# Attention and SwiGLU block: the low part of the first chunk's row maxima is made by an accumulated TensorE product, and the later units' subtract stands farther from its neighbours

## The chip, the cores and the metric

The kernel runs on one core of one Trainium2 chip. Its engines work side by side, each in the order of its own instructions: TensorE (PE, with its weight loads as PEld), VectorE (DVE), ScalarE (ACT), GpSimd (POOL) and SyncE (SP, which here only starts DMAs). The metric is the device time of one execution in microseconds (us), as the median of several runs.

## What is computed

A transformer block over 2048 tokens of width 512: adaptive layer norm, attention with 32 heads of 16 values each and a full softmax, and a SwiGLU feed-forward of width 1792, each with a gated residual.

```python
mod = (_silu(c) @ w_mod).reshape(c.shape[0], 6, 1, -1)
sa, ca, ga, sb, cb, gb = (mod[:, 0], mod[:, 1], ..., mod[:, 5])
h = _layernorm(x) * (1 + ca) + sa
q, k, v = split_heads(h @ wqkv)              # H = 32, Dh = 16
p = _softmax(einsum("bhqd,bhkd->bhqk", q, k) * Dh ** -0.5)
x = x + ga * (merge_heads(p @ v) @ wo)
h = _layernorm(x) * (1 + cb) + sb
x = x + gb * ((_silu(h @ w_gate) * (h @ w_up)) @ w_down)
```

The weights are scaled so that scores are large; the softmax subtracts each row's maximum, and products are made from a high and a low part of each operand (a value rounded to TensorE's fp32r format, and the rest), which keeps about full fp32 accuracy.

## The kernel before

**Units and steps.** The 2048 queries are four chunks of 512. A unit is one chunk and one group of four heads, so there are 32 units, 8 to a chunk; the first chunk's are units 0 to 7. A unit has 16 steps, one for each tile of 128 keys, and a step has four pairs. A pair (`pair_of`) is one score product of the current unit (L512, 128 keys by 512 queries, into one PSUM bank), its exponential on ScalarE (L514), and one product for a later unit's maxima (L482, 128 queries by 512 keys), of which VectorE takes the row maximum (L484). The maxima run 23 steps (`LEAD`) ahead of the scores. After a step follow the products with V (L527).

**The maxima of a unit.** When all 64 row maxima of unit u are there, `max_rows(u)` runs. A small reduce on VectorE (L489) brings the four key parts together into the tile `m`, 128 by 16. ScalarE rounds `m` into the first half of `nm` (L501), VectorE subtracts the rounded value from `m` into the second half (L502). Both inputs of this subtract lie in SBUF. TensorE turns the 32 columns into rows and negates them by a product with `minus`, a negated identity (L494); ScalarE copies the rows out (`mr`, L496), and two DMAs on SP's queue (L498) put them into rows 48 and 49 of the operand `qop` of unit u. The operand `kop` holds ones there, so the score product subtracts the maximum by itself, as a high and a low part.

**What sets the order.** There is no scheduler here: the order is written out by hand. `max_rows` appends its later pieces to the list `side`, and each pair takes one piece off it after its own products; `wait` is an empty piece. So the number of empty pieces is the distance, in pairs, between the reduce, ScalarE's rounding, the subtract and the row product. The last piece appends the row product to `tails`, which is emptied by `flush`. In the part written by `plain` that is after every three pairs (`WIN`); in the part written by `filled`, where feed-forward products (L733) are placed between the pairs, it is after a block of 10 or 5 pairs.

**The stages.** Until about 200 us the projections are made. Then come 144 plain steps (`STARTS[0]`), in which the first chunk's units are done; only units 1 to 8 are of interest there, since the maxima run ahead. In these steps GpSimd also splits the weights of the feed-forward and of `wo` into high and low parts (`split_weights`, L585 to L593 and L611, L627): it loads them, works on tiles of 128 by 512 or 1024 and stores them by DMA. After that the output projection and feed-forward of the chunks before are filled in between the pairs.

**SP's queue** takes its DMAs in order, and each waits for what it needs: the rows (L498), key operands (`kop<-kd`, L414), query operands (`qop<-qd`, L414), the softmax denominators (L538 to L548) and the feed-forward weights (`wgu<-gu_dr`, L668).

Of the kernel before, what the change touches and what calls it, by code (L numbers as in the profile page):

```python
# [9 lines left out]
F32 = mybir.dt.float32  # L10
# [4 lines left out]
ALU = mybir.AluOpType  # L15
AX = mybir.AxisListType
# [3 lines left out]
P = 128  # L20
# [7 lines left out]
NC = 4  # L28
# [9 lines left out]
LEAD = 23  # L38
# [4 lines left out]
UG = 16 * NG  # L43
# [61 lines left out]
def block_kernel(ctx, tc, x, wqkv, wo, w_gate, w_up, w_down, c, w_mod, out):  # L105
    nc = tc.nc
# [27 lines left out]
    ident = const.tile([P, P], F32, name="ident")  # L134
    eps_t = const.tile([P, 1], F32, name="eps_t")
    minus = const.tile([P, P], F32, name="minus")
# [322 lines left out]
    pb = ctx.enter_context(tc.tile_pool(name="pb", bufs=2, reuse_waits="tile"))  # L459
    kop[1] = [pb.tile([P, 2, CW], F32R, name=f"kop1{c}", bufs=1) for c in range(NC)]  # L460
    pf = None
    nms = [pb.tile([P, 2, 16], F32R, name=f"nm{e}", bufs=1) for e in range(2)]
    qop, mx, pts, pv, o_, due, res = {}, {}, {}, {}, {}, {}, {}
    posts, tails = [], []
    n = 16 * NU
# [19 lines left out]

    def max_rows(u):

        m = pb.tile([P, 16], F32, name="m", tag="m")
        nc.vector.tensor_reduce(m, mx.pop(u).rearrange("p b s t f -> p (b s t) f"), op=ALU.max, axis=AX.X)  # L489
        nm = nms[u % 2]  # L490

        def rows():
            pr = bank("pr")[0:32, 0:P]
            nc.tensor.matmul(pr, nm.rearrange("p r h -> p (r h)").bitcast(F32), minus, start=True, stop=True)  # L494
            mr = pb.tile([32, P], F32R, name="mr", tag="mr", bufs=1)
            nc.scalar.copy(mr, pr)  # L496
            for r in range(2):
                nc.sync.dma_start(qop[u][KR + r:KR + r + 65:64].bitcast(F32), mr[16 * r:16 * r + 16, :].bitcast(F32))  # L498

        wait = lambda: None  # L500
        side.extend([wait] * 3 + [lambda: nc.scalar.copy(nm[:, 0, :], m), wait,  # L501
                                  lambda: nc.vector.tensor_sub(nm[:, 1, :].bitcast(F32), m, nm[:, 0, :].bitcast(F32)),  # L502
                                  wait, lambda: tails.append(rows)])

    def score(i, h):
        u, kt = divmod(i, 16)
# [318 lines left out]
    side = []  # L825
# [61 lines left out]
    def after(i):  # L887
        nonlocal pf
        for f in due.pop(i, []):
            f()  # L890
        j = i + LEAD
        if j % 16 == 15 and j < n:
            max_rows(j // 16)
        if i == -2:
            run(late)
            sm.finish()
            es_a0.close()
            pf = ctx.enter_context(tc.tile_pool(name="pf", bufs=1, side="right", reuse_waits="tile"))
            load_q(2)
        if 0 <= i < UG and i % 16 in (3, 5, 8):  # L900
            next(weights2, None)
# [195 lines left out]
```

## Time and profile before

| what | us |
| --- | --- |
| median of 3 runs (1903.62 to 1907.65) | 1906.04 |
| the profiled execution | 1910.84 |
| its span | 1909.1 |
| L484 on DVE, 2048 row maxima, busy | 1261.8 |
| L482 on PE, their products, busy | 788.5 |
| L512 on PE, the score products, busy | 744.4 |

The span is what the profiler saw from the first to the last instruction; the profiled execution's time holds another 1.74 us around it. A group's row in the profile names the line of the code, the engine, the operation, what it writes and reads, the count, and then busy time, mean duration of one in ns, and idle time of the engine just ahead of it with what ended it. A row of the timeline is start, duration, engine, line. A row of windows is the stretch, its length, and then the busy time of an engine in it with the number of instructions, the clock granted to TensorE (1.00 is full), the share of the DMA engines and their GB/s.

### The profile page before, as it was taken

How to read it: one execution, taken by the hardware profiler on the slowest of the kernel's cores; microseconds unless marked ns; L12 is line 12 of the kernel's file. 1: busy time of each engine (PE TensorE's matmuls, PEld its weight loads, DVE VectorE, ACT ScalarE, POOL GpSimd, SP SyncE). 2: the span in 40 equal slices, each digit the busy share in tenths (PEclk: the TensorE clock that was granted, in tenths of full speed). 3: DMA queues.
4: the chain of work that ended last, by engine and by line, in shares of the span. 5: the costliest groups of instructions: out<-in, count | busy, mean ns of one | idle time of the engine just before them, and what ended most of it. 6: DMA issues, size and time to landing. Idle time of an engine off the chain costs nothing.

```text
span 1909.1 us, 42023 instructions
## 1 busy us (share of the span) xinstructions
PE 1861.7 (98%) x16872; PEld 1209.6 (63%) x16872; DVE 1492.1 (78%) x2515; ACT 1253.3 (66%) x2406; POOL 486.1 (25%) x528
## 2 busy tenths in 40 slices
PE   7999999999999999999999999999999999999999
PEld 5766444444455677777765677766664677666887
DVE  5459999999998888888888888888788888821543
ACT  4221888787786777777777777777777777784211
POOL 3000544454501222212232222222223222232200
PEclk9999999998999999999999999999999999999999
DMA  8854555554432433333244333333242433333543
GB/s 280 289 210 131 183 179 177 160 172 157 156 130 68 132 116 124 116 111 120 92 146 120 105 112 115 122 119 120 79 131 77 148 116 111 118 124 143 195 182 109
DMA packets 101787, 266.97 MB, mean 140 GB/s; under 512 B 20360, under 2 KB 25480, under 8 KB 88408
## 3 DMA queue, kind: packets, MB, share of 16 engines
q1 hardware_dynamic: 86984, 202.27, 33.4%
q0 software_dynamic: 14608, 62.01, 9.2%
q8 instruction: 133, 2.18, 0.5%
q14 instruction: 62, 0.51, 0.1%
HBM read 201.46 MB, written 61.86 MB: 138 GB/s over the span
## 4 chain that ended last, share of the span: by engine, by line
PE 78%; DVE 20%; ACT 1%; DMA 1%; issue 0%; SPq 0%; ACTq 0%; DVEq 0%
PE bank L527 19%; PE bank L733 18%; DVE mx L484 17%; PE bank L512 14%; PE bank L482 9%; PE bank L742 7%; PE bank L219 7%; DVE nm L502 1%; PE bank L775 1%; DMA kop<-kd 0%; PE bank L172 0%; DMA wm_ab<-in_w_mod 0%; PE bank L494 0%; PE bank L718 0%; DVE stt L758 0%
## 5 line engine op out<-in xcount | busy, mean ns | idle before, releaser
L484 DVE TENSOR_REDUCE mx<-bank 128x1 f32<-128x512 f32 x2048 | 1261.8, 682 | 199.6 <-PE bank L482 153.4
L482 PE MATMUL bank<-kop,qop 48*128 48x512 f32 x2048 | 788.5, 446 | 4.8 <-DMA qop<-qd 1.6
L512 PE MATMUL bank<-qop,kop 50*128 50x512 f32 x2048 | 744.4, 424 | 4.6 <-DVE mx L484 2.6
L512 PEld LDWEIGHTS bank<-qop,kop 50*128 50x128 f32 x2048 | 352.4, 187 | 245.6 <-issue 40.3
L482 PEld LDWEIGHTS bank<-kop,qop 48*128 48x128 f32 x2048 | 348.5, 186 | 70.4 <-DVE mx L484 15.4
L733 PE MATMUL bank<-act,wgu 64*128 64x512 f32 x1872 | 353.9, 398 | 0.0
L733 PEld LDWEIGHTS bank<-act,wgu 64*128 64x128 f32 x1872 | 228.2, 186 | 20.7 <-ACT part L808 4.1
L733 PE MATMUL bank<-wd,mid 64*128 64x512 f32 x912 | 151.4, 394 | 0.0
L809 POOL TENSOR_TENSOR x<-part,x 128x512 f32<-128x512 f32 x76 | 96.4, 1287 | 194.3 <-ACT part L808 194.3
L554 POOL TENSOR_TENSOR on<-o,rb 128x512 f32<-128x512 f32 x31 | 39.8, 1285 | 362.4 <-DMA rb<-d_dr 318.1
L794 POOL CAST mid<-m 128x512 fp32r<-128x512 f32 x40 | 24.4, 610 | 352.6 <-PE bank L482 198.7
L733 PEld LDWEIGHTS bank<-wd,mid 64*128 64x128 f32 x912 | 97.9, 186 | 13.5 <-DVE m L792 2.0
L219 PE MATMUL bank<-hT,wqs 128*128 128x512 f32 x384 | 96.1, 400 | 2.3 <-ACT hT L338 1.0
L790 DVE SCALAR_TENSOR_TENSOR q<-th,bank 128x512 f32<-128x512 f32 x56 | 38.1, 681 | 72.1 <-ACT th L786 72.1
L219 PEld LDWEIGHTS bank<-hT,wqs 128*128 128x128 f32 x384 | 70.3, 188 | 24.2 <-issue 6.0
L786 ACT ACTIVATE th<-bank 128x512 f32<-128x512 f32 x56 | 33.5, 598 | 77.8 <-PE bank L742 65.9
L379 DVE TENSOR_TENSOR prt<-bank,prt 128x512 fp32r<-128x512 f32 x32 | 22.0, 689 | 46.8 <-ACT prt L377 42.7
L377 ACT CAST prt<-bank 128x512 fp32r<-128x512 f32 x32 | 18.8, 587 | 59.7 <-PE bank L219 52.8
L792 DVE TENSOR_TENSOR m<-bank,q 128x512 f32<-128x512 f32 x56 | 38.7, 692 | 24.5 <-PE bank L742 21.6
L742 PE MATMUL bank<-act,kop 128*128 128x512 f32 x240 | 57.2, 396 | 0.0
L733 PE MATMUL bank<-wgu,act 64*128 64x512 f32 x288 | 55.0, 397 | 0.1
L742 PE MATMUL bank<-wd,mid 128*128 128x512 f32 x216 | 52.3, 395 | 0.3 <-DVE mid L795 0.3
(6276 smaller groups left out, 5198.7 us busy)
## 6 DMA issues: line engine op xcount, KB each, us to landing
kop<-kd SPq DMA_DIRECT2D x256, 192.0 KB
wgu<-gu_dr SPq DMA_DIRECT2D x46, 1024.0 KB
wd<-wd_dr SPq DMA_DIRECT2D x28, 1024.0 KB
gu_dr<-wgu POOLq DMA_DIRECT2D x14, 1024.0 KB, 5.4
qop<-qd SPq DMA_DIRECT2D x64, 192.0 KB
kop<-gu_dr SPq DMA_DIRECT2D x20, 512.0 KB
kd<-prt SPq DMA_DIRECT2D x16, 512.0 KB
qd<-prt SPq DMA_DIRECT2D x16, 512.0 KB
```

The costliest lines, as they stand in the source:

```text
L219: nc.tensor.matmul(pt, lhs(a, k), rhs(b, k), start=(n == 0), stop=(n == 3 * nk - 1))
L482: nc.tensor.matmul(pm, qop[u][rows, s, qt * P:(qt + 1) * P], kop[u % 2][kc][rows, s, :], start=True, stop=True)
L484: nc.vector.tensor_reduce(mx[u][:, b, s, qt, kc:kc + 1], pm, op=ALU.max, axis=AX.X)
L512: nc.tensor.matmul(sp, kop[u % 2][kt // 4][rows, h // 2, kt % 4 * P:(kt % 4 + 1) * P], qop[u][rows, h // 2, :], start=True, stop=True)
L527: nc.tensor.matmul(pv[u][32 * h:32 * h + 32, cols], v_flat[:, e0:e0 + 32], p_[h][:, cols], start=(kt == 0 and half == 0), stop=(kt == 15), ...
L554: mul.tensor_mul(on, o, rb)
L733: nc.tensor.matmul(outs[e], lhs(e, a, k)[rows], rhs(b, k)[rows], start=(ph == 0 and j == 0), stop=(ph == 1 and j == z))
L742: nc.tensor.matmul(outs[e], lhs(e, a, k), rhs(b, k), start=(j == 0), stop=(j == z))
L786: nc.scalar.activation(th, outs[0], AF.Tanh, scale=0.5)
L790: nc.vector.scalar_tensor_tensor(q, th, 1.0, outs[0], op0=ALU.add, op1=ALU.mult)
L792: nc.vector.tensor_mul(m32, outs[1], q)
L809: nc.gpsimd.tensor_add(ch.x2[:, t, :], part, ch.x2[:, t, :])
```

## The change

For units 0 to 8 (`early`), the subtract on VectorE is left out. The reduce writes `m` twice, side by side (128 by 32, its input read twice); ScalarE writes the rounded value into the second half of `nm`, whose first half is zero from two memsets ahead; and TensorE accumulates two products into the same rows, `m` by `minus` and `nm` by `ident`. So the first 16 rows are minus the maximum, the others the rounded value less the maximum. For units 9 to 31 the subtract stays; ScalarE's rounding and the subtract stand one pair earlier, and the row product one pair later.

```diff
     nms = [pb.tile([P, 2, 16], F32R, name=f"nm{e}", bufs=1) for e in range(2)]
+    for t in nms:
+        nc.vector.memset(t[:, 0, :].bitcast(F32), 0.0)
...
-        m = pb.tile([P, 16], F32, name="m", tag="m")
-        nc.vector.tensor_reduce(m, mx.pop(u).rearrange("p b s t f -> p (b s t) f"), op=ALU.max, axis=AX.X)
+        m = pb.tile([P, 2, 16], F32, name="m", tag="m")
+        by_head = mx.pop(u).rearrange("p b s t f -> p (b s t) f")[:, None]
         nm = nms[u % 2]
+        early = 16 * u + 15 - LEAD < UG
+        wait = lambda: None
...
-            nc.tensor.matmul(pr, nm.rearrange("p r h -> p (r h)").bitcast(F32), minus, start=True, stop=True)
+            parts = ((m, minus), (nm.bitcast(F32), ident)) if early else ((nm.bitcast(F32), minus),)
+            for k, (a, by) in enumerate(parts):
+                nc.tensor.matmul(pr, a.rearrange("p r h -> p (r h)"), by, start=k == 0, stop=k == len(parts) - 1)
...
-        wait = lambda: None
-        side.extend([wait] * 3 + [lambda: nc.scalar.copy(nm[:, 0, :], m), wait,
-                                  lambda: nc.vector.tensor_sub(nm[:, 1, :].bitcast(F32), m, nm[:, 0, :].bitcast(F32)),
-                                  wait, lambda: tails.append(rows)])
+        if early:
+            nc.vector.tensor_reduce(m, by_head.to_broadcast([P, 2, 16, NC]), op=ALU.max, axis=AX.X)
+            side.extend([wait] * 3 + [lambda: nc.scalar.copy(nm[:, 1, :], m[:, 0, :])] + [wait] * 3)
+        else:
+            nc.vector.tensor_reduce(m[:, 0, :], by_head[:, 0], op=ALU.max, axis=AX.X)
+            side.extend([wait] * 2 + [lambda: nc.scalar.copy(nm[:, 0, :], m[:, 0, :]), wait,
+                                      lambda: nc.vector.tensor_sub(nm[:, 1, :].bitcast(F32), m[:, 0, :],
+                                                                   nm[:, 0, :].bitcast(F32))] + [wait] * 3)
+        side.append(lambda: tails.append(rows))
```

VectorE's order at unit 4, before: `mx` is the tile of maxima, the banks are those of the L482 products, and the tile `nm_974` is `nm` of the even units.

```order
L489 TENSOR_REDUCE m<-mx 128x16
L484 TENSOR_REDUCE mx<-bank_65 128x1
L484 TENSOR_REDUCE mx<-bank_66 128x1
L484 TENSOR_REDUCE mx<-bank_63 128x1
L484 TENSOR_REDUCE mx<-bank_64 128x1
L484 TENSOR_REDUCE mx<-bank_65 128x1
L484 TENSOR_REDUCE mx<-bank_66 128x1
L502 TENSOR_TENSOR nm_974<-m,nm_974 128x16
L484 TENSOR_REDUCE mx<-bank_63 128x1
```

And the same place in the changed kernel, where the maxima's line is L486 and the small reduce's is L507:

```order
L507 TENSOR_REDUCE m<-mx 128x32
L486 TENSOR_REDUCE mx<-bank_65 128x1
L486 TENSOR_REDUCE mx<-bank_66 128x1
L486 TENSOR_REDUCE mx<-bank_63 128x1
L486 TENSOR_REDUCE mx<-bank_64 128x1
L486 TENSOR_REDUCE mx<-bank_65 128x1
L486 TENSOR_REDUCE mx<-bank_66 128x1
L486 TENSOR_REDUCE mx<-bank_63 128x1
```

The subtract is gone, and the row maxima of the next products follow each other without it; the small reduce writes 32 columns in place of 16. On TensorE, the row product of unit 4 before stands behind the last product of a window and ahead of the products with V (L527):

```order
L512 MATMUL bank_69<-qop,kop_973 128x512
L482 MATMUL bank_65<-kop_970,qop 128x512
L494 MATMUL bank_67<-minus,nm_974 32x128
L527 MATMUL bank_70<-pt__3263,v_flat 32x256
```

In the changed kernel the score product's line is L523, the row product's L500 and the products with V are L538:

```order
L523 MATMUL bank_69<-qop,kop_973 128x512
L484 MATMUL bank_65<-kop_970,qop 128x512
L500 MATMUL bank_67<-minus,m 32x128
L500 MATMUL bank_67<-ident,nm_974 32x128
L538 MATMUL bank_70<-pt__3265,v_flat 32x256
```

The place is the same; there are two row products, and neither reads anything that a subtract wrote. In the filled part the extra pair moves the row product of units 15 and 23 past the end of a block, by 10 pairs, and that of unit 30 by 5; the other units' stay where they were. On SP's queue at unit 15, before, the rows (`qop<-mr`) go ahead of a weight load and two key operands:

```order
L548 DMA rb<-d_dr 128x1x512
L498 DMA qop<-mr 2x8x128 x2
L668 DMA wgu<-gu_dr 128x2048
L414 DMA kop_89<-kd 48x2x512 x2
L414 DMA kop_90<-kd 48x2x512 x2
```

In the changed kernel (L559 is the denominators' broadcast, L679 the weight load, L504 the rows):

```order
L559 DMA rb<-d_dr 128x1x512
L679 DMA wgu<-gu_dr 128x2048
L414 DMA kop_89<-kd 48x2x512 x2
L504 DMA qop<-mr 2x8x128 x2
L414 DMA kop_90<-kd 48x2x512 x2
```

The rows go behind the weight load and the first key operand now. GpSimd's order is unchanged.

## The prediction

> **What bounds the kernel now.** I read the page first, then the stage in which the removed instruction stands, cut into units.
>
> ```profile
> span 1909.1 us, 42023 instructions
> ...
> PEclk9999999998999999999999999999999999999999
> ...
> PE 78%; DVE 20%; ACT 1%; DMA 1%; issue 0%; SPq 0%; ACTq 0%; DVEq 0%
> PE bank L527 19%; PE bank L733 18%; DVE mx L484 17%; PE bank L512 14%; PE bank L482 9%; PE bank L742 7%; PE bank L219 7%; DVE nm L502 1%; PE bank L775 1%; DMA kop<-kd 0%; PE bank L172 0%; DMA wm_ab<-in_w_mod 0%; PE bank L494 0%; PE bank L718 0%; DVE stt L758 0%
> ```
>
> On the whole TensorE sets the end (78% of the chain of waits), but a fifth of the chain is VectorE's, nearly all of it row maxima (L484). Two things stand out: the subtract L502, 32 instructions of 128 by 16, has 1% of the chain, and the granted clock, full elsewhere, has a lower tenth in the first quarter of the span. In the chain in order of time, VectorE's long pieces stand between 200 and 560 us, such as
>
> ```profile
> 306.15 27.00 DVE mx L484 x45
> ...
> 344.13 3.11 DVE nm L502
> ```
>
> So I cut that stretch at the starts of the small reduce L489, from unit 1's at 219.73 to unit 9's at 553.58: each window is one unit's worth of pairs, and holds the subtract of the unit whose reduce opens it. This is VectorE in each, with the clock behind the count:
>
> ```profile
> 219.73:257.88 38.15, 38.15 (x67) 1.00 0.42 129
> 257.88:297.94 40.06, 39.92 (x68) 1.00 0.68 209
> 297.94:340.34 42.40, 42.32 (x70) 1.00 0.58 176
> 340.34:383.86 43.52, 41.46 (x67) 0.96 0.55 171
> 383.86:423.85 39.99, 39.85 (x68) 1.00 0.57 184
> 423.85:471.80 47.95, 43.23 (x69) 0.86 0.49 156
> 471.80:514.46 42.66, 40.15 (x68) 0.92 0.50 166
> 514.46:553.58 39.12, 38.99 (x68) 1.00 0.44 146
> sum 333.85, DVE 324.07; mean DVE 40.51
> ```
>
> The reader is to see that VectorE is busy for 324 of 333.85 us, so it sets the pace here, and that the units should be alike but last from 38.2 to 48.0 us. The same windows for the subtract alone, four of them and the sum:
>
> ```profile
> 219.73:257.88 38.15, 0.33 (x1) 1.00 0.42 129
> 257.88:297.94 40.06, 1.83 (x1) 1.00 0.68 209
> ...
> 383.86:423.85 39.99, 1.76 (x1) 1.00 0.57 184
> ...
> 514.46:553.58 39.12, 0.90 (x1) 1.00 0.44 146
> sum 333.85, DVE 15.77; mean DVE 1.97
> ```
>
> One subtract takes 2 us on the mean. The timeline of unit 4 shows why:
>
> ```profile
> 344.04 0.78 POOL L585 DMA_DIRECT2D mid<-in_B_w_up  x1
> 344.05 3.18 DVE L502 TENSOR_TENSOR nm<-m,nm 128x16 f32<-128x16 f32 x1
> 344.83 2.36 POOL L627 TENSOR_TENSOR mid<-mid,gb_bc 128x1024 f32<-128x1024 f32 x1
> 347.15 1.28 DVE L484 TENSOR_REDUCE mx<-bank 128x1 f32<-128x512 f32 x2
> ...
> 347.37 0.35 PE L494 MATMUL bank<-minus,nm 128*32 128x128 f32 x1 [3.19 <-DVE nm L502]
> ```
>
> The subtract begins beside GpSimd's work and ends at 347.23, 0.04 us after GpSimd's L627 (347.19): it was held by it. VectorE's queue stands behind it, and TensorE, which has reached the row product L494, waits 3.19 us. Then the clock falls, here behind the subtracts of units 4, 6 and 7:
>
> ```profile
> 348.00:352.00 4.00, 4.00 (x34) 0.65 0.35 69
> ...
> 432.00:436.00 4.00, 4.00 (x25) 0.50 0.49 143
> ...
> 480.00:484.00 4.00, 4.00 (x26) 0.51 0.61 216
> ```
>
> At half the clock TensorE no longer feeds VectorE, which idles in turn:
>
> ```profile
> L484 DVE TENSOR_REDUCE mx<-bank 128x1 f32<-128x512 f32 x511 | 309.0, 680 | 9.7 <-PE bank L482 7.8 <-PE bank L512 1.4
> ```
>
> **The change, part by part.** *The subtract of units 1 to 8 goes.* I take its worth from whole units, since it also brings the idle time after it. The four units at full clock throughout, less their subtract, last 38.15 - 0.33 = 37.82, 40.06 - 1.83 = 38.23, 39.99 - 1.76 = 38.23 and 39.12 - 0.90 = 38.22 us; their mean is 38.13. (Unit 3, 42.40, is at full clock too, but its subtract was a long one and TensorE lagged behind it; it is no clean unit.) Eight such units make 305.0 us. What is late next: VectorE's own reduces, which no longer wait for anything; in the clean units TensorE kept up with them at the pace that all would then have.
>
> *The small reduce is twice as wide.* The narrow one begins at 514.46 and the next reduce at 514.59, beside a GpSimd instruction:
>
> ```profile
> 514.46 0.21 DVE L489 TENSOR_REDUCE m<-mx 128x16 f32<-128x64 f32 x1
> 514.59 1.88 DVE L484 TENSOR_REDUCE mx<-bank 128x1 f32<-128x512 f32 x3
> ...
> 514.46 1.28 POOL L554 TENSOR_TENSOR on<-o,rb 128x512 f32<-128x512 f32 x1 [13.62 <-DMA rb<-d_dr]
> ```
>
> So it takes 0.13 us of VectorE's time. The doubled one isn't in this trace; it costs between nothing and another whole duration, 0.21 us, more. I take one more step, 0.13, since a second pass over the same tile is the nearest row: 8 times 0.13 is 1.0 us (0 to 1.7). The same rows show that the narrow reduce isn't held while GpSimd works on SBUF.
>
> *Two more passes on TensorE.* The row product is recorded as two passes, and the second product adds as many.
>
> ```profile
> L494 PE MATMUL bank<-minus,nm x16: 269/270/421, 223.9 to 519.3; 128*32 128x128 f32 x16
> ```
>
> A unit's two passes follow 0.11 us apart and last 0.27 each, so a unit's cost is 0.38 us at most, 3.0 for eight. What hides it is TensorE's wait for VectorE; without that cover it costs up to 3.0. I take 0, since in the clean units VectorE idled for 0.14 us at most. The row products now need ScalarE's rounding only, which stood two pairs ahead of the subtract and isn't moved here.
>
> *One key load stays late.* In unit 4 TensorE waited about 1 us at the end of
>
> ```profile
> 364.32 8.13 DMA kop<-kd
> ```
>
> That load collided with GpSimd's weight stores and will meet them again somewhere; I leave 1.0 us in (0 to 4, one such wait for each second unit).
>
> *Two memsets* stand ahead of a subtract of the projections, where VectorE has idle time:
>
> ```profile
> 121.19 0.69 DVE L379 TENSOR_TENSOR prt<-bank,prt 128x512 fp32r<-128x512 f32 x1 [1.59 <-ACT prt L377]
> ```
>
> Two writes of 16 columns fit into 1.59 us: 0; without the cover at most two of the small reduces, 0.4. Unit 0's subtract (0.18 us) goes too: 0.
>
> *Units 9 to 31.* The subtract stays, and TensorE seldom waits for it: from 553.58 to 1700 us only
>
> ```profile
> PE bank L494 <- DVE nm L502: 0.9, 2, 0.7
> ```
>
> Moved apart, this is worth 0 to 0.9; I take 0. The price of the distance is the row product of units 15, 23 and 30, which comes later (below, the last rival).
>
> **The sum.** The stretch becomes 305.0 + 1.0 + 1.0 = 307.0 us in place of 333.85: 26.9 less, say 27. From below: 15.8 of subtracts and 9.7 of idle time, less the 1.0 that stays and the 1.0 of the wider reduce, is 23.5; the other 3.4 are reduces that ran late behind the stalls of units 3 and 6 without a recorded wait. I take the clean units, which are measured whole. The rest of the span, 1355 us, begins earlier by as much and is bound by TensorE, so nothing takes it back. The profiled execution (1910.84 with its span of 1909.1) then comes to 1883.9. It lies 4.8 us above the median of the runs, so against the median, 1906.04, I forecast **1879 us**.
>
> **The rivals.** *The clock still falls.* If the low clock has another cause than these waits, the 9.7 us of idle time and the late reduces stay, and the gain is 15.8 - 1.0 = 14.8: 1891 us. For it: unit 3's subtract, 2.60 us, left the clock at 1.00, while unit 7's, 2.06, was followed by 0.51. Against it: the clock is full in all four units whose subtract took under 2 us, and each fall begins within 4 us of a wait for L494. 8%. [...]
>
> *The wider reduce is held as the subtract was* (the change doesn't do what it says). Then nine reduces stall where nine subtracts did, and the time stays at about 1906. Against it: the reduce beside L554 above, and the small reduces all take about 0.2 us. For it: only that it reads SBUF while GpSimd works. 4%.
>
> *The late rows, price small or large.* In unit 15's place before:
>
> ```profile
> 861.65 0.30 PE L494 MATMUL bank<-minus,nm 128*32 128x128 f32 x1
> ...
> 862.98 1.13 SPq L498 DMA_DIRECT2D qop<-mr  x2
> ...
> 869.09 0.39 PE L512 MATMUL bank<-qop,kop 50*128 50x512 f32 x1
> ...
> 875.67 0.39 PE L512 MATMUL bank<-qop,kop 50*128 50x512 f32 x1
> ```
>
> The row product moves from 861.65 to behind the score at 869.09, and unit 15's first score, which needs the rows, is the one at 875.67. From the row product to the end of the DMA's issue took 2.46 us, so it would be issued by about 871.9, and 3.8 us are left for it to land. The nearest landing in the trace is
>
> ```profile
> o_dr<-on POOLq DMA_DIRECT2D x31, 256.0 KB, 2.4
> ```
>
> and the farthest is the 8.13 us of the key load above. At 2.4 nothing waits; at 8.13 TensorE waits 4.3 us, and then the clock falls as behind unit 6, where 47.95 - 3.10 - 38.13 = 6.7 us were lost after the wait. That is 11 us for a place. At one or two places the result is 1884 to 1901, still faster than before: 5%. **It is slower than before** when all three places (units 15, 23 and 30) pay 11 us: 33 - 27 = 6, so 1912 us. It decides from a wait of over 3.5 us at each of the three, since 3 times (3.5 + 6.7) is above 27; unit 30 has more room (11 pairs in place of 6 from row product to score), which speaks against. 3%.
>
> **How the numbers follow.** The forecast has the other 80%. Its own spread: all eight units like the quickest, 37.82, make the gain 30 us, with 0.9 from the later units 31, and the runs before reach 2.4 us below their median: 1873. At the other end stands the clock rival, 1891, which also takes in the 3.0 of TensorE's passes and the 4 of key loads; with a little of the runs' spread the range is 1873 to 1892. Left out are the two rivals at 1906 and 1912 and half of the small price: about 1 in 10. A measurement of this kernel can tell about 0.2%, 3.8 us, from no change. Faster: 80 + 8 + 5 = 93%; within 0.2%: 4%; slower: 3%.
>
> **What would show it.** Right: the eight windows from unit 1's small reduce to unit 9's last 38.0 to 38.6 us each with the clock at 1.00; no VectorE instruction of 16 or 32 columns there takes over 0.4 us; TensorE's wait ahead of the row products is gone; the small reduce takes about 0.3 us; the stretch behind unit 9's reduce is as long as before, 1355 us. Wrong: long windows with a low clock though no subtract is there; a small reduce of 1 us or more; TensorE waiting for the DMA of the rows at the first score of units 15, 23 or 30; the key loads holding TensorE in more units than one.

## The result, and the profile after

| | before | changed |
| --- | --- | --- |
| median of 4 runs each, us | 1905.20 | 1888.26 |
| range of the runs, us | 1903.62 to 1907.65 | 1886.52 to 1888.99 |
| profiled execution, us | 1910.84 | 1888.41 |
| its span, us | 1909.1 | 1886.6 |

The ratio is 0.9909 with a 95% interval of 0.9891 to 0.9926: by the medians 16.9 us faster, where 27 were forecast. The time of 1888.26 lies inside the range of 1873 to 1892. Two later sets of runs of the same two kernels, e7 and e10 below, gave ratios of 0.9886 and 0.9892, some 20 to 22 us. Two executions of the study, one of e3 (2426.15 us) and one of the kernel before in e0's group (1993.78 us), were slow ones and stand outside every ratio.

The page of the changed kernel, its span, the granted clock in 40 slices and the chain of waits by engine and by line:

```profile
span 1886.6 us, 42054 instructions
...
PEclk9999999999999999999999999999999999999999
...
PE 92%; DVE 5%; ACT 1%; DMA 1%; issue 0%; SPq 0%; ACTq 0%; DVEq 0%
PE bank L538 25%; PE bank L523 20%; PE bank L744 19%; PE bank L484 12%; PE bank L753 8%; PE bank L219 7%; DVE mx L486 4%; PE bank L786 1%; PE bank L500 1%; PE bank L172 0%; DMA wm_ab<-in_w_mod 0%; PE bank L729 0%; DVE stt L769 0%; PE bank L289 0%; DMA qop<-qd 0%
```

The lower tenth in the clock is gone, the subtract has left the chain, and VectorE's share of it fell from 20% to 5%. That is more than the time shows. The chain passes back and forth between two engines that are both nearly always busy in this stage (TensorE for 309.26 us of 309.92, VectorE for 308.40), and a share of it is no saving. The same windows as before, from unit 1's small reduce to unit 9's, VectorE in each, with the clock behind the count:

```profile
218.27:256.25 37.98, 37.98 (x67) 1.00 0.44 127
256.25:294.69 38.44, 38.25 (x66) 1.00 0.65 215
294.69:334.99 40.30, 39.82 (x68) 1.00 0.60 185
334.99:372.97 37.98, 37.98 (x66) 1.00 0.63 199
372.97:411.43 38.46, 38.26 (x67) 1.00 0.55 182
411.43:451.77 40.34, 39.88 (x68) 1.00 0.63 196
451.77:489.75 37.98, 37.98 (x67) 1.00 0.58 181
489.75:528.19 38.44, 38.25 (x66) 1.00 0.48 153
sum 309.92, DVE 308.40; mean DVE 38.55
```

The stage went from 333.85 to 309.92 us, 23.9 less, and the clock is full in all eight units. They are still not alike: 37.98, 38.44 and 40.30 repeat with a period of three. VectorE has the same work per instruction everywhere and idles little, as the groups of this stage show (the row maxima and the small reduce; busy time and mean ns of one, then idle time ahead and its releasers):

```profile
L486 DVE TENSOR_REDUCE mx<-bank 128x1 f32<-128x512 f32 x511 | 307.6, 694 | 1.2 <-PE bank L484 0.9
L507 DVE TENSOR_REDUCE m<-mx 128x32 f32<-128x128 f32 x8 | 2.4, 297 | 0.2
```

So the longest units hold more row maxima. In the written order of VectorE, before and after alike, 63, 63 and 66 of them stand between two small reduces in turn, since `max_rows` is called only at the end of a window of three pairs and 64 is not a multiple of three. Units 3 and 6 have the 66. At 0.6 us each, three more maxima are 1.8 us of the 2.1 by which these two are longer than the mean of the others; most of the rest is idle time of VectorE (40.30 less 39.82). Why units of 63 differ among themselves by 0.46 us was not taken apart.

TensorE's waits in the stage, with their total, number and longest in us, are now only these:

```profile
PE bank L500 <- ACT pt__2819 L525: 0.2, 1, 0.2
PE bank L500 <- ACT pt__4334 L525: 0.2, 1, 0.2
```

The wait for the subtract is gone, and so, in this execution, is the one for a key load. At unit 4, where the subtract of before was held for 3.18 us, the timeline now has:

```profile
334.99 0.31 DVE L507 TENSOR_REDUCE m<-mx 128x32 f32<-128x128 f32 x1
335.19 5.50 DVE L486 TENSOR_REDUCE mx<-bank 128x1 f32<-128x512 f32 x9
...
340.27 2.40 POOL L638 TENSOR_TENSOR mid<-mid,gb_bc 128x1024 f32<-128x1024 f32 x1
```

GpSimd still works at this place, and nothing on VectorE stops for it; the wide reduce costs VectorE 0.20 us from its start to the next one's. Behind unit 9's small reduce, the windows of TensorE's, its loads', VectorE's, ScalarE's and GpSimd's busy time, of before and of after, one row each:

```profile
553.58:1909.10 1355.52, 1342.99 (x12766) 922.60 (x12764) 1020.16 (x1717) 906.63 (x1732) 311.30 (x354) 1.00 0.37 120
```

```profile
528.19:1886.60 1358.41, 1346.64 (x12765) 923.62 (x12764) 1019.22 (x1717) 906.70 (x1732) 310.88 (x354) 0.99 0.37 119
```

Here the changed kernel takes 2.9 us more. With 1.5 us less ahead of unit 1's reduce the profiles differ by 1.5 + 23.9 - 2.9 = 22.5 us. The runs differ by only 16.9, because the profiled execution of before was 5.6 us above the median of its runs, and that of after 0.15.

### The profile page after: what moved, and what is told of

Read it like the earlier page. It is cut to its first block, busy times and chain, and to the rows that moved or that the text cites. A ratio compares the mean times of both kernels' runs of the same rounds, so it can differ in the third digit from the quotient of the medians.

```text
span 1886.6 us, 42054 instructions
## 1 busy us (share of the span) xinstructions
PE 1857.2 (98%) x16890; PEld 1209.3 (64%) x16890; DVE 1475.3 (78%) x2508; ACT 1252.0 (66%) x2406; POOL 485.7 (26%) x528
## 4 chain that ended last, share of the span: by engine, by line
PE 92%; DVE 5%; ACT 1%; DMA 1%; issue 0%; SPq 0%; ACTq 0%; DVEq 0%
PE bank L538 25%; PE bank L523 20%; PE bank L744 19%; PE bank L484 12%; PE bank L753 8%; PE bank L219 7%; DVE mx L486 4%; PE bank L786 1%; PE bank L500 1%; PE bank L172 0%; DMA wm_ab<-in_w_mod 0%; PE bank L729 0%; DVE stt L769 0%; PE bank L289 0%; DMA qop<-qd 0%
## 5 line engine op out<-in xcount | busy, mean ns | idle before, releaser
L486 DVE TENSOR_REDUCE mx<-bank 128x1 f32<-128x512 f32 x2048 | 1260.8, 687 | 193.5 <-PE bank L484 148.2
L523 PE MATMUL bank<-qop,kop 50*128 50x512 f32 x2048 | 739.5, 421 | 4.0 <-DVE mx L486 1.8
L523 PEld LDWEIGHTS bank<-qop,kop 50*128 50x128 f32 x2048 | 349.8, 185 | 241.3 <-issue 35.0
```

The lines of the kernel that those rows point to most:

```text
L486: nc.vector.tensor_reduce(mx[u][:, b, s, qt, kc:kc + 1], pm, op=ALU.max, axis=AX.X)
L523: nc.tensor.matmul(sp, kop[u % 2][kt // 4][rows, h // 2, kt % 4 * P:(kt % 4 + 1) * P], qop[u][rows, h // 2, :], start=True, stop=True)
```

## The experiments

Eleven runs were made, in three groups; those of a group share a chip and its runs of the kernel before, whose medians were 1908.12 us (e0, e1, e2, e7), 1907.45 (e3 to e6) and 1905.83 (e8 to e10). "Stage" is the time from unit 1's small reduce to unit 9's, "behind" the span after it, both from the profile of that run. "Subtracts" are the eight of units 1 to 8 together.

| run | median, us | ratio to before (95%) | stage | subtracts | behind |
| --- | --- | --- | --- | --- | --- |
| before, as profiled above | 1905.20 | | 333.85 | 15.8 | 1355.5 |
| e0, before again | 1904.47 (1 run) | | 331.91 | 11.1 | 1353.4 |
| e1, first chunk only | 1885.14 | 0.9881 (0.9862 to 0.9899) | 311.41 | none | 1353.5 |
| e2, later units only | 1908.82 | 1.0014 (0.9997 to 1.0031) | 336.50 | 14.0 | 1360.3 |
| e7, the change again | 1886.24 | 0.9886 (0.9867 to 0.9905) | 309.87 | none | 1355.8 |
| e3, split moved | 1895.82 | 0.9939 (0.9922 to 0.9956) | | | |
| e4, idle subtract | 1897.31 | 0.9956 (0.9938 to 0.9974) | 318.75 | 9.1 | 1358.2 |
| e5, far everywhere | 1907.97 | 1.0008 (0.9991 to 1.0025) | 327.10 | 13.9 | 1357.7 |
| e6, change and split moved | 1887.15 | 0.9894 (0.9876 to 0.9912) | 309.86 | none | 1354.8 |
| e8, split moved again | 1894.55 (1 run) | | 319.34 | 4.5 | 1355.4 |
| e9, first chunk only again | 1883.22 | 0.9877 (0.9854 to 0.9900) | 309.85 | none | 1353.8 |
| e10, the change again | 1886.01 | 0.9892 (0.9871 to 0.9913) | 310.07 | none | 1356.7 |

**e0, the kernel before once more.** No edit.

> The kernel before, unchanged, to see a second profile of it. Its first profiled execution took 1910.84 us, 5.6 above the median of its runs (1905.2). Theory A (the lost time behind the subtracts differs from one execution to the next): in an execution nearer the median the subtracts of units 1 to 8 again take 14 to 17 us together, but the stretch from unit 1's small reduce to unit 9's is 326 to 331 us in place of 333.85, with VectorE idle for 3 to 7 us in place of 9.7, and the units with a low clock need not be 4, 6 and 7. Rival B (the stretch is the same in each execution, and the 5 us lie in the rest of the span): the stretch is 333 to 335 us, and what follows unit 9's reduce is 1350 in place of 1355.5.

Three of its eight windows and their sum, and the groups of the row maxima and of the subtract in this stage:

```profile
298.48:341.75 43.27, 42.05 (x69) 0.96 0.55 174
341.75:385.83 44.08, 40.50 (x67) 0.92 0.54 167
...
469.26:507.72 38.46, 38.46 (x67) 1.00 0.58 181
sum 331.91, DVE 319.24; mean DVE 39.90
```

```profile
L484 DVE TENSOR_REDUCE mx<-bank 128x1 f32<-128x512 f32 x511 | 308.8, 679 | 12.6 <-PE bank L482 9.9 <-PE bank L512 2.6
L502 DVE TENSOR_TENSOR nm<-m,nm 128x16 f32<-128x16 f32 x8 | 11.1, 1381 | 0.0
```

The subtracts of the same program took 11.1 us here and 15.8 in the first profile, and other units were hit. In unit 6, held for 3.10 us before, the subtract slipped in just ahead of GpSimd's load:

```profile
429.62 0.17 DVE L502 TENSOR_TENSOR nm<-m,nm 128x16 f32<-128x16 f32 x1
429.71 0.78 POOL L585 DMA_DIRECT2D mid<-in_B_w_up  x1
```

It began 0.09 us ahead of the load here and 0.09 us behind it in the first profile (427.57 and 427.48). So which subtracts were held varied between these two executions. The loss of the stage is there each time: 333.85 and 331.91 us, and 336.50 in e2, whose units 1 to 8 are those of before, against 310. Less time in subtracts did not mean less idle time: 12.6 us of it stand here beside 11.1, where 3 to 7 were expected, and 9.7 beside 15.8 in the first profile.

**e1 and e2, the two parts of the change apart.** e1 is the changed kernel with the later units' distances as they were:

```diff
-            side.extend([wait] * 2 + [lambda: nc.scalar.copy(nm[:, 0, :], m[:, 0, :]), wait,
+            side.extend([wait] * 3 + [lambda: nc.scalar.copy(nm[:, 0, :], m[:, 0, :]), wait,
...
-                                                                   nm[:, 0, :].bitcast(F32))] + [wait] * 3)
+                                                                   nm[:, 0, :].bitcast(F32)), wait])
```

> The changed kernel, with units 9 to 31 put back to the distances of before (rounding at the fourth place, subtract at the sixth, row product at the eighth). Theory A (all of the gain comes from units 0 to 8; the spacing of the later units is worth nothing either way): ratio to before 0.990 to 0.993, the same as the whole change within 0.2%. Rival B (the later row products of units 15, 23 and 30 give back the 2.9 us by which the rest of the span grew): faster than the whole change by 2 to 4 us, ratio about 0.989. Rival C (the spacing helps the later units): slower than the whole change by over 2 us.

e2 is the kernel before with the wider distance for units 9 to 31 alone:

```diff
-        side.extend([wait] * 3 + [lambda: nc.scalar.copy(nm[:, 0, :], m), wait,
+        far = 16 * u + 15 - LEAD >= UG
+        side.extend([wait] * (3 - far) + [lambda: nc.scalar.copy(nm[:, 0, :], m), wait,
...
-                                  wait, lambda: tails.append(rows)])
+                                  ] + [wait] * (1 + 2 * far) + [lambda: tails.append(rows)])
```

> The kernel before, with only the second half of the change: in units 9 to 31 rounding and subtract one pair earlier and the row product one pair later; units 0 to 8 as before. Theory A (spacing worth nothing): ratio 0.999 to 1.001. Rival B (late rows cost): 1.001 to 1.003, and TensorE waits for the DMA of the rows at the first score of units 15, 23 or 30. Rival C (spacing helps): 0.997 to 0.999.

e7 is the change itself on the same chip.

> The changed kernel, unchanged, on the same chip as the other runs of this call, so that the parts can be compared with the whole. Expected 0.990 to 0.993 of before. A second profile of it also says whether the 2.9 us that the rest of the span grew by come again: theory A (the phase of the clock at one chunk's start) says the sum of the units behind unit 9 differs by 2 to 3 us from profile to profile; rival B (the spacing) says that it is 1358 us again.

The first chunk's part alone gives the whole gain (0.9881, beside 0.9886 of the change); the distance alone gives nothing (1.0014, its interval reaching from 0.9997 to 1.0031). In e1 a key load did hold TensorE for 1.5 us, and unit 6 took 41.90 us where e7 has 40.38; the stage is longer by the same 1.5.

**e4, VectorE's hold without TensorE's wait.** The changed kernel, with a subtract put back on VectorE in its old place, writing a tile that nobody reads:

```diff
+    idle = pb.tile([P, 16], F32, name="idle", bufs=1)
...
-            side.extend([wait] * 3 + [lambda: nc.scalar.copy(nm[:, 1, :], m[:, 0, :])] + [wait] * 3)
+            side.extend([wait] * 3 + [lambda: nc.scalar.copy(nm[:, 1, :], m[:, 0, :]), wait,
+                                      lambda: nc.vector.tensor_sub(idle, m[:, 0, :], nm[:, 1, :].bitcast(F32)), wait])
```

> The changed kernel with VectorE's subtract of units 0 to 8 put back at its place, but into a tile that nothing reads: the row product doesn't wait for it. Theory A (the loss starts with VectorE's queue standing behind the held subtract): the subtracts take 13 to 17 us together, the stretch of units 1 to 8 is 323 to 334 us in place of 310, ratio 0.995 to 1.001. Rival B (the loss comes from TensorE waiting at the row product, which alone reads the result): the stretch is 310 to 314 us and the ratio 0.987 to 0.991, though the subtracts take as long. If the clock stays at 1.00 with the stretch at about 325, the row product's wait is what lowers the clock.

Unit 7's window, the sum of the eight, and the two groups in the stage:

```profile
456.42:497.78 41.36, 40.07 (x68) 0.96 0.52 170
...
sum 318.75, DVE 316.38; mean DVE 39.55
```

```profile
L487 DVE TENSOR_REDUCE mx<-bank 128x1 f32<-128x512 f32 x511 | 307.4, 677 | 2.3 <-PE bank L485 1.7 <-PE bank L525 0.6
L510 DVE TENSOR_TENSOR idle<-m,nm 128x16 f32<-128x16 f32 x8 | 9.1, 1140 | 0.0
```

The hold itself is there with no reader, as at unit 2 in the timeline, where TensorE's row product goes ahead beside it:

```profile
260.36 0.41 PE L501 MATMUL bank<-minus,m 128*32 128x128 f32 x2
260.38 2.69 DVE L510 TENSOR_TENSOR idle<-m,nm 128x16 f32<-128x16 f32 x1
260.66 2.37 POOL L640 TENSOR_TENSOR mid<-mid,gb_bc 128x1024 f32<-128x1024 f32 x1
```

Subtracts of 9.1 us lengthen the stage by 318.75 - 309.92 = 8.83, less than the 13 us or more that were expected if the hold made the whole loss, and more than the 4 or less if TensorE's wait did. That a hold costs its own length holds for the sum only. Units 2, 5 and 8, with subtracts of 2.69, 2.11 and 1.56 us, are each longer than in the changed kernel by 0.46 us less than the subtract, so a part of a hold is made up again. Unit 7, with 2.10, is 3.4 longer: there VectorE was late by enough that TensorE waited 1.00 us for row maxima, and the clock fell, as its 0.96 shows. Elsewhere the clock stayed at 1.00, and behind the subtracts VectorE idled 2.3 us, where e0 with subtracts of 11.1 idled 12.6. So most of the idle time and of the low clock of before came with TensorE's wait at the row product; a hold alone brought a little of it.

**e5, distance in place of removal.** The kernel before with the wider distance for all units (the edit of e2 with `far = True`).

> The kernel before, with the later units' spacing used for all 32: rounding and subtract one pair earlier, the row product one pair later, the subtract kept. Theory A (VectorE is held wherever the subtract stands): the subtracts of units 1 to 8 take 12 to 18 us together, the stretch is 326 to 334 us, less than before only by what TensorE's waits at the row product cost, ratio 0.996 to 1.001. Rival B (distance is enough): the stretch is 310 to 316 us, ratio 0.987 to 0.992.

TensorE's wait at the row product, and the groups of the stage:

```profile
PE bank L494 <- DVE nm L503: 10.6, 6, 2.4
```

```profile
L484 DVE TENSOR_REDUCE mx<-bank 128x1 f32<-128x512 f32 x511 | 307.8, 676 | 5.9 <-PE bank L482 5.9
L503 DVE TENSOR_TENSOR nm<-m,nm 128x16 f32<-128x16 f32 x8 | 13.9, 1742 | 0.0
```

Two more pairs between subtract and row product did not free TensorE: it still waited six times, 10.6 us in all. Idle time fell by more than half against e0 and the stage to 327.10, but the subtracts were no shorter, and the median is that of before.

**e3, e6 and e8, the same cure from GpSimd's side.** The splitting of the weights is moved to other steps of each unit, in the kernel before (e3, e8) and in the changed one (e6):

```diff
-        if 0 <= i < UG and i % 16 in (3, 5, 8):
+        if 0 <= i < UG and i % 16 in (0, 3, 14):
```

> The kernel before, subtract and all, with GpSimd's pieces of the weight split started at steps 0, 3 and 14 of a unit in place of 3, 5 and 8, so that GpSimd has little to do when the subtract comes (step 9 or 10). Theory A (GpSimd's work holds the subtract): the subtracts of units 1 to 8 take 0.2 to 0.4 us each, 1.3 to 3 us together in place of 14 to 16, the stretch from unit 1's small reduce to unit 9's is 308 to 313 us, the clock there is 1.00, ratio 0.986 to 0.992, as the change itself. Rival B (the subtract is slow in this stage for a reason of its own, such as the full queue of reduces): it still takes about 2 us each and the ratio is 0.999 to 1.001.

> The changed kernel with GpSimd's pieces also moved to steps 0, 3 and 14. Theory A (the subtract was the only victim of GpSimd's work): the same as the change, ratio 0.986 to 0.992, the stretch 308 to 312 us. Rival B (GpSimd's work also costs something by its DMAs, which share the engines with the key loads): 2 us or more faster than the change and than the kernel before with the pieces moved.

e3's profile is that of its execution of 2426 us, at a granted clock of 0.66 throughout, and can't be set beside the others; e8 ran the same kernel once more.

> The kernel before with GpSimd's weight splitting moved to other steps of each unit, once more, for a profile of its stage. If the gain of 0.6% measured for it comes from subtracts that no longer meet GpSimd's work, about half of units 1 to 8 have a subtract of 0.2 us and the sum of the eight is 5 to 8 us in place of 11 to 16; the stage is 318 to 324 us, and idle time of VectorE 3 to 6 us. If the subtracts are as long as before (11 us or more) and the stage is still under 325 us, the gain has another source, such as the key loads meeting GpSimd's stores less often; then TensorE's waits for L494 are as before and those for kop are gone.

Moving the collision alone is worth 0.6% (e3), less than the 0.8 to 1.4% expected, since some subtracts still met GpSimd's work: one took 2.23 us in e8. In the changed kernel it is worth nothing (0.9894, beside 0.9909, 0.9886 and 0.9892 of the change): there is no subtract left to collide. In e8 the subtracts fell to 4.5 us and the stage to 319.34, with 7.2 us of idle time (3 to 6 were expected). One unit shows the clock apart from the subtracts. TensorE in four pieces of unit 3, cut where the granted clock changes and at the same distance around, and its longest wait in the unit:

```profile
323.94:327.35 3.41, 3.10 (x33) 1.00 1.03 266
327.35:330.76 3.41, 1.29 (x13) 1.00 1.07 293
330.76:334.17 3.41, 3.41 (x26) 0.50 1.01 426
334.17:337.58 3.41, 3.41 (x40) 1.00 0.33 125
```

```profile
PE bank L482 <- DMA kop<-kd: 2.4, 1, 2.4
```

This unit's subtract took 0.16 us, yet the unit took 43.78, 3.4 more than the 40.3 to 40.5 it takes in the changed kernel. TensorE waited 2.4 us for a key load, and right behind that the clock was 0.50 for 3.41 us. So in this unit no subtract lowered the clock; it fell behind a wait of TensorE.

**e9 and e10, does the distance cost?** e1 and the change again, side by side.

> The change with the later units' old distances, on the same chip as the change itself in the next run. If the wider distance of units 9 to 31 costs the 2 to 3 us that the profiles so far have behind unit 9's reduce, this kernel is 1 to 3 us faster than the next; if it is worth nothing, the two medians lie within 1.5 us of each other. Stage 310 to 311 us in both.

> The change itself, beside the run ahead: 1885 to 1889 us, stage 310 us; the stretch behind unit 9's reduce 1355 to 1359 us.

Over both groups the ten runs without the wider distance (e1, e9) have a mean of 1884.05 us, the ten with it (e7, e10) 1886.14: 2.1 us apart, 95% interval 0 to 4.2. The profiles say the same. The stretch behind unit 9's reduce is 1353.4 to 1355.5 us in all five profiles without the distance (before, e0, e1, e8, e9) and 1354.8 to 1360.3 in the seven with it, means 1354.3 and 1357.4. By units, each from its small reduce to the next, in us:

| unit | five without | seven with |
| --- | --- | --- |
| 10 | 46.95 to 48.37 | 47.39 to 50.27 |
| 13 | 51.34 to 51.41 | 51.43 to 51.51 |
| 18 | 46.96 to 48.35 | 47.64 to 50.49 |
| 24 | 52.50 to 52.54 | 51.66 to 51.71 |

Most of the excess stands in units 10 and 18, eight units apart; in unit 24 the distance gains. In unit 18 a low clock stood already in the profile of before, and in that of the changed kernel a longer stretch of it (windows of TensorE, its loads, VectorE, ScalarE and GpSimd, of before and then of after):

```profile
1023.80:1028.66 4.86, 4.76 (x33) 2.09 (x35) 4.54 (x10) 2.04 (x4) 3.15 (x15) 0.80 0.74 261
1028.66:1033.52 4.86, 4.86 (x42) 2.06 (x41) 3.91 (x7) 3.63 (x8) 2.70 (x4) 0.85 0.00 0
```

```profile
1000.31:1005.36 5.05, 4.62 (x32) 1.73 (x26) 4.55 (x10) 1.88 (x4) 2.79 (x14) 0.73 0.68 226
1005.36:1010.41 5.05, 5.05 (x36) 2.19 (x36) 2.84 (x5) 2.57 (x6) 3.03 (x4) 0.59 0.02 3
```

In both units it is the low clock that makes the spread. At full clock they take 46.9 to 47.0 us without the distance and 47.4 to 47.7 with it; a stretch at 0.50 of 3.41 us adds 1.4, one of 6.83 us 2.6 to 2.9. Such stretches stand in 3 of these 10 units without the distance, all of 3.41 us, and in 8 of the 14 with it, seven of them of 6.83. So about 1 us of the excess is there in every execution, and the rest comes and goes with the clock. Why the distance brings these stretches more often and makes them longer stays open; no run took it apart. The fastest kernel of the study is e1/e9, the first chunk's part alone; on the medians it isn't clearly apart from the change.

## Why the prediction was right, and where its size was off

**Right: the cause.** The gain lies in units 1 to 8, the clock there is 1.00, no VectorE instruction of 16 or 32 columns takes over 0.31 us, and TensorE's wait ahead of the row products is gone. The split into a hold (15.8 us) and an aftermath of idle time and low clock (9.7) is borne out by e4: with the hold alone the stage lost 8.8 us for 9.1 of subtracts, and all but one short stretch of low clock was gone. VectorE's busy time in the stage fell by 15.7 us and its idle time by 8.3.

**Wrong: the size of the clean units.** The step that failed is that "the units should be alike", from which eight clean units of 38.13 us were made 305.0. All four clean units were ones of 63 row maxima. Two of the eight have 66, and at 0.6 us each (307.6 us over 511) three more are 1.8 us a unit, 3.6 in all. The stage came to 309.92 us where the sum had 307.0. The 3.4 us of "reduces that ran late behind the stalls of units 3 and 6 without a recorded wait" were these: units 3 and 6 are the two with 66, and this part of their length was work and not a stall. The other sum, from below, had 23.5; measured were 23.9.

**Wrong by the same kind of choice: the execution.** This is the largest term. The offset of 4.8 us was carried over, as if the changed kernel's profile would lie as far above its runs; it lay 0.15 above. The profiled execution of before was a long one. Of the 9.3 us between 1879 and 1888.26, 4.7 are this offset, 2.9 the stage, 2.9 the stretch behind unit 9, less 1.5 that were gained ahead of unit 1; the rest is rounding. Against e0, at 1904.47, the three profiles of the change (means 218.79 to unit 1, 309.95 in the stage, 1356.95 behind) give -1.5 + 22.0 - 3.5 = 17.0 us. That this is the gain of the first runs is chance, since e0 was one of the shorter executions on its chip, where the median of before was 1908.12 and the change gained some 22. So the stage is worth 22 to 27 us, by the execution of before that it is set against, and the whole change 17 to 22.

**Wrong: the later units at 0.** They were to gain 0 to 0.9; they lose some 2 us by the medians (0 to 4.2) and 3 by the profiles. The rival that spoke of them had another mechanism, TensorE waiting for the rows at units 15, 23 and 30. No such wait is in the trace of the changed kernel.

**The small terms.** The wider reduce takes 0.20 us in place of 0.13, so 0.6 for eight, where 1.0 was set. The key load, 1.0 set, cost nothing in the first profile and 1.5 in e1's. TensorE's extra passes and the memsets show no wait: 0, as set.

**The range held partly by luck.** Its upper end, 1892, was made for a clock that still falls, TensorE's passes and more key loads. None of these came in the profile; what used up the room was the offset, the stage and the later units.

**The rivals.** That the clock still falls is refuted for this stage: 1.00 in eight units. In e8 the clock fell to 0.50 behind a wait of 2.4 us for a key load. What spoke for this rival, that unit 3's subtract of 2.60 us left the clock at 1.00 while unit 7's of 2.06 did not, goes with where the two waits fell on the grid of time in the last section: unit 3's gave 1.26 and 1.36 us of idle time in two intervals, unit 7's 1.50 in the one ahead of the fall. That the wider reduce is held as the subtract was is refuted too, but not by the mean of 297 ns, since seven of the eight reduces of that profile met no work of GpSimd's. It is refuted by unit 1's: in e10 it began at 218.84 beside GpSimd's L601 (`wgu<-mid,wgu`, 218.75 to 220.04) and took 0.27 us, and so it was beside the same instruction in e7, e6 and e9.

## What to carry to other kernels

Before clean units are summed up, count the instructions in each: a stage written in windows of another size than its units gives units of unequal work, and the surplus looks like a stall. Work out a gain against more than one execution of before, where a stall depends on which of two engines comes first. And a short instruction that another engine held up cost about its hold here (8.8 us for 9.1 in e4), but with TensorE waiting for its result about as much again (11.1 us of hold and 12.6 of idle time in e0), so first look at who waits for it; here distance was no cure (1.0008 in e5) and removal was (0.9881 in e1).

## What the runs showed of the hardware

**In these profiles the clock fell behind waits of TensorE as short as 1.07 us, and where a wait fell in time went with it.** In every profile here but e3's the granted clock is either 1.00 or 0.50, and a low stretch lasts 3.41 us or a whole multiple of it (3.41, 6.83 and 13.65 us in before; the one at a profile's end is cut off), in each of these executions on one grid of 3.41 us; values between are means over a window that holds both. Three cuts along this grid show TensorE's busy time and then the clock: unit 3 of before, whose wait of 2.61 us was split by an edge, unit 4 of before, whose wait of 3.19 us was not, and unit 8 of e8, with a wait of 1.07 us at the row product.

```profile
299.64:303.05 3.41, 2.16 (x23) 1.00 0.34 91
303.05:306.46 3.41, 2.05 (x24) 1.00 0.39 141
```

```profile
344.02:347.43 3.41, 0.21 (x6) 1.00 0.70 207
347.43:350.84 3.41, 3.41 (x24) 0.50 0.18 44
```

```profile
498.02:501.43 3.41, 2.34 (x19) 1.00 0.20 64
501.43:504.84 3.41, 3.41 (x24) 0.50 0.30 97
```

Over the stage in the twelve profiles without e3's, counting those intervals of the grid that ran at full clock, the clock fell at the end of all 17 in which TensorE was idle for more than 1.5 us, of 6 of the 18 with 1.0 to 1.5, and of none of the other 1043. So no fall came behind the wait of 2.61 us, 1.26 and 1.36 in two intervals, nor behind e1's 1.54 for a key load (0.50 and 1.05), while one came behind 1.07 in one interval. In before alone it fell at the end of the intervals with 3.19, 1.64 and 1.50 us of idle time and not of those with 1.47, 1.36, 1.26, 1.08, 1.04 and 1.02. This is a count over profiles and no run was made to test it; what decides between 1.0 and 1.5 us stays open.

**Undisturbed units repeat closely.** Units 1, 4 and 7 took 37.96 to 37.99 us in all three profiles of the change (units 3 and 6 40.30 to 40.53), so differences of 0.1 us a unit, such as unit 13's above, can be read from a few profiles.
